# Three loads of second token weights are issued ahead of the last row loads, in the prologue of a Fourier filter with an MLP mixer

## The chip, the cores and the metric

The kernel runs on one core of one Trainium2 chip, as a single launch. The metric is the device time in microseconds (us), the median of several executions. A core has five engines, each with its own instruction queue that is worked off in order: PE (matmuls, with weight loads shown as PEld), DVE (elementwise), ACT (elementwise, and it issues DMAs), POOL (elementwise, and it issues DMAs) and SP (it only issues DMAs). They wait for one another through semaphores. DMAs run beside them on 16 DMA engines; an issued DMA "lands" when its semaphore is set.

## What is computed

Inputs are x of 8 x 3008 x 256 and the weights, all 64-bit floats; the result is 32-bit. Cut to what matters:

```
y = irfft(rfft(x, axis=1) * (filt_r + 1j * filt_i))      # per batch and channel, 3008 points
xt = y.transpose(0, 2, 1)
h  = relu(xt @ w_tok1) @ w_tok2                          # 3008 -> 256 -> 3008, along the tokens
u  = y + h.transpose(0, 2, 1)
out = u + relu(u @ w_ch1) @ w_ch2                        # 256 -> 1536 -> 256, along the channels
```

## The kernel before

**Stages.** The transform of 3008 points is done as matmuls: step A with 64 points (`a_unit`), step B with 47 points (`b_unit`, L529), the product with the filter, and back (`bi_unit`, L553), whose results are stored to the DRAM tensor `g_tmp` (L571, issued by ACT). `t4_load` (L608) loads them back as rows, six tiles per batch. The token mixer multiplies all six with `w1` (`token_sums`, L613, matmuls of L617), applies the relu (`token_relu`, L629) and multiplies with `w2` (`u_unit`, L642, matmuls of L647). The channel mixer (`mix`, L846) then runs for eight batches, with the filter of the next batches woven in. Batch 0 is filtered first, alone, in the prologue; the prologue ends where the mixer starts, about 153 us into a span of 2573.1 us.

**The weights.** They arrive as 64-bit floats and are turned into 32-bit ones on the chip, in 38 tiles: 0 to 11 hold `w_tok1`, 12 to 25 hold `w_tok2` (L329; tiles 18 and 25 have 188 columns, the others 471, and 128 partitions of 8 bytes a number), 26 to 37 hold the channel weights. Each tile passes four steps, in the order of the tiles: *begin* (the load into a staging buffer `st`, L337, issued by POOL), *copy* (ACT, L262), *middle* (DVE, L264 and L265), *end* (DVE, L268 and L270, after which the staging buffer is free; for tiles 12 to 17 PE then sums the two halves by L303 and L304 and ACT copies them out by L306, for later tiles DVE sums them by L292). `convert_middle` (L411) does one middle, and then issues the PE sums that are left; `convert_end` (L415) does one end, the copies that are due, and calls `fill(5)`: it begins tiles until there are five more begun than ended. While the list `pause` is not empty, `fill` begins none.

**The order around the change.** The order on each engine is that in which the program is written. The loop at L937 runs the filter of batch 0; each of its steps k does one middle or one end (L952 to L957) and some row loads, as their part of `g_tmp` becomes ready. From k = 27 on the loads are paused (L951); 18 tiles (0 to 17) are begun by then. The loop leaves with 16 tiles ended and 17 middles done. Then stand the last row loads (L967 and L968): the last 16 rows of each of the six tiles, 64 KB each, three on SP and three on POOL. They wait for the last store to `g_tmp`. Then the pause is lifted (L969), and the loop at L974 goes on with the tiles: i = 16 does middle 17, end 16, and begins tiles; i = 17 does middle 18, end 17, begins a tile, and then writes the PE sums that are left (`sum_up`) and `token_sums(0)`. So on DVE the first half of tile 18 (L264, L265) stands ahead of the second half of tile 17 (L268, L270), and on PE the sums of tile 17 (L304) stand ahead of `token_sums`. After the loop come `token_relu` and `u_unit` (L980 to L984).

**Buffers.** Tiles 18, 19 and 20 are staged in the buffers that tiles 12, 13 and 14 used, so their loads wait for L270 of those tiles. Tiles 21 to 25 follow in the buffers of 15 to 19.

Of the kernel before, what the change touches and what calls it, by code (L numbers as in the profile page):

```python
# [127 lines left out]
def kernel(  # L128
# [273 lines left out]
    def sum_up():  # L402
        while behind:
            behind.pop(0)()

    def convert():

        convert_middle()
        convert_end()

    def convert_middle():  # L411
        advance(middle)
        sum_up()

    def convert_end():  # L415
        ended[0] += 1
        advance(end)
        copies()
        fill(5)
# [3 lines left out]
    def copies():  # L423

        while copied[0] < len(tiles) and copied[0] <= ended[0] + (copied[0] < len(tiles) - len(LAST)):
            advance(copy)
            copied[0] += 1

    begun, pause = [0], []

    def fill(ahead):
        while not pause and begun[0] < len(tiles) and begun[0] < ended[0] + (4 if begun[0] >= len(tiles) - len(LAST) else ahead):
            start()

    def start():
        advance(begin)
        begun[0] += 1
# [26 lines left out]
    def rows_of(t_d, b):  # L464
        return t_d[b].rearrange("k (g a) d -> (k g) a d", a=A)
# [142 lines left out]
    def t4_load(b, c, lo=PARTS[0], hi=P, queue=nc.sync):  # L608
        if lo == 0:
            t4[b, c] = t4p.tile([P, TC4, D], FP32, tag="t4", name="t4")  # L610
        queue.dma_start(t4[b, c][lo:hi], rows_of(g_d, b)[lo:hi, ts(c, TC4), :])

    def token_sums(b):  # L613
        acc = bank(free_bank()).rearrange("p (t d) -> p t d", t=TC)
        for a in range(A):
            for t in range(TC):
                nc.tensor.matmul(acc[:, t, :], w1[:, a, ts(t, P)], t4[b, a // TC4][:, a % TC4, :],  # L617
                                 start=(a == 0 and t == 0), stop=(a == A - 1 and t == TC - 1))
        return acc

    def token_relu(b, acc):
        if b:
            h1 = w2[:, 0:1, 7 * 256:].rearrange("p o (s t) -> p o s t", t=P)[:, :, 0:7, :]
            for t, to in enumerate((slice(0, 5, 4), slice(1, 7, 5))):
                nc.scalar.activation(out=h1[:, 0, to, :], in_=acc[:, t].rearrange("p (e i) -> p e i", e=DH), func=AF.Relu)
            combine(h1)
            return h1[:, 0]
        h1 = h1p.tile([P, TC, D], FP32, tag="h1", name="h1")
        nc.scalar.activation(out=h1, in_=acc, func=AF.Relu)  # L629
        return h1  # L630
# [194 lines left out]
    def u_part(b, m, i):  # L825
        if i == 0:
            uts[b, m] = up.tile([P, DH, 512], FP32, tag="u", name="u")
        (u_quarter if b else u_unit)(b, m, h1s[b], uts[b, m], i)

    def v_steps(b, m):  # L830
        vts[b, m] = vp.tile([P, 4, 256], FP32, tag="v", name="v")
        t13, t2, t4_ = u_sums(uts[b, m], vts[b, m], width(m))

        def t24():
            t2()
            t4_()

        return [t13, t24]
# [91 lines left out]
    with tc.manual_schedule():  # L930
        nc.sync.dma_start(wa0, wa0_d)
        nc.vector.memset(turned[:, A:K2, :], 0.0)
        for t in filts:
            nc.vector.memset(t, 0.0)
        half = 0
        second = dft(GROUPS[1])
        for i, _ in enumerate(dft(GROUPS[0])):  # L937
            if i == 0:
                nc.scalar.dma_start(wai_t, wait_d)
            k = i - NXC - 2  # L940

            if i < NXC:
                if i in (1, 3, 5, 7, 9):
                    start()
                if i == NXC - 1:
                    copies()
                    for t, src in ((wa, wa_d), (wai, wai_d), (ident, ident_d)):
                        nc.scalar.dma_start(t, src)
            elif k >= 0:
                if k == K2 - 5:  # L950
                    pause.append(True)  # L951
                while half < 2 * IN_B * (k + 1) // K2:  # L952
                    if half % 2:
                        convert_end()
                    else:
                        convert_middle()
                    half += 1  # L957

                if 19 <= k < 25:
                    t4_load(0, k - 19, 0, PARTS[1])  # L960
                elif 26 <= k < 29:
                    for c in range(2):
                        t4_load(0, 2 * (k - 26) + c, PARTS[1], PARTS[2])
                elif k in (30, 31):
                    for c in range(3):
                        t4_load(0, 3 * (k - 30) + c, PARTS[2], PARTS[3])
        for c in range(A // TC4):  # L967
            t4_load(0, c, PARTS[3], P, (nc.sync, nc.gpsimd)[c % 2])  # L968
        pause.clear()  # L969
        both = wcp.tile([P, 2, JP, 7, P], FP32, tag="wc", name="wc")  # L970

        chan.extend((both[:, 0], both[:, 1]))
        next(second)
        for i in range(IN_B, A // 2 + TC * W2G):  # L974
            convert()
            if i == A // 2 + BY_PE - 1:
                sum_up()
                acc = token_sums(0)

        ahead[0](XF, nc.gpsimd)  # L980
        h1s[0] = token_relu(0, acc)
        for dh in range(DH):
            convert()
            u_part(0, 0, dh)  # L984
        for f in v_steps(0, 0):
            f()
        for _ in range(XB):
            next(second)
        group, todo, done = -1, iter(()), True

        def next_ready(b):
            return done or b != GROUPS[group][-1]

        left, places, at, spread = K2 + 3, 2 * 24, 0, True
        for b, i, place in mix(next_ready):
            if group + 1 < len(GROUPS) and b == GROUPS[group + 1][0]:
                if not done:
                    raise AssertionError("the filter's steps don't fit beside the mixer's")  # L1000
                group += 1
                done = group + 1 == len(GROUPS)
                todo = iter(()) if done else dft(GROUPS[group + 1]) if group else second
            due = place == 1
            if group == 0:
                due = spread
                if not spread and place:
                    at += 1
                    due = at * left // places > (at - 1) * left // places or at > places
            if due and not done:  # L1010
                spread = next(todo, "end")
                done = spread == "end"
# [30 lines left out]
```

## Time and profile before

| what | value |
|---|---|
| median of 9 runs | 2577.27 us (2572.84 to 2579.93) |
| profiled execution | 2575.04 us, of which its span is 2573.1 us |
| PE busy | 2490.7 us, 97% of the span |
| DVE busy | 1920.1 us, 75% |
| ACT, POOL busy | 680.0 us, 592.0 us |
| mean granted PE clock | 0.992 |
| DMA | 248.37 MB, 97 GB/s on average; 220 GB/s between 60 and 180 us |

The span is the time from the first to the last instruction. Three more views are used below. The chain of waits follows the work that ended last back, at each step to what released it; its lines are start, duration and what. The timeline lists each engine's instructions: start, duration, engine, line of the code, operation, output<-input and shape, and in brackets the idle time before it and who ended that. The table of windows gives, for each stretch of time, its length, the busy time (and count) of PE, PEld, DVE, ACT and POOL, then the granted PE clock, the mean busy share of the DMA engines, and GB/s.

### The profile page before, as it was taken

What the parts mean: (1) busy time and instruction counts of PE and PEld (TensorE: products, weight loads), DVE (VectorE), ACT (ScalarE), POOL (GpSimd) and SP (SyncE); (2) the same over time, 40 slices, a digit from 0 to 9 for tenths busy, and PEclk for the clock granted to TensorE, in tenths of its full rate; (3) what the DMA queues carried; (4) which work ended last, traced back from release to release, by engine and by line L of the source; (5) the groups of instructions that cost most, each with busy time, mean ns of one, the idle gap of its engine ahead of it and who ended that gap; (6) DMA issues with size and microseconds to landing.
All of it is one profiled execution on the core that took longest, in us unless ns stands there. A gap on an engine that the chain in (4) does not pass through costs nothing.

```text
span 2573.1 us, 32285 instructions
## 1 busy us (share of the span) xinstructions
PE 2490.7 (97%) x11204; PEld 2050.3 (80%) x11204; DVE 1920.1 (75%) x3594; ACT 680.0 (26%) x1342; POOL 592.0 (23%) x1073
## 2 busy tenths in 40 slices
PE   7889999999999999999999999999999999999997
PEld 3567666888888777898888777898888888898887
DVE  7687888567686998756776899856788587757776
ACT  5633222122221222222221222212222122212222
POOL 5573322212111121112121111211211121211222
PEclk8999999999999999999999999999999999999999
DMA  9873434333332333213332343213333222111100
GB/s 222 233 211 125 136 113 130 105 110 101 124 103 80 91 107 87 78 56 120 101 109 86 89 119 96 89 33 110 101 105 94 66 76 71 40 32 37 43 14 20
DMA packets 166432, 248.37 MB, mean 97 GB/s; under 512 B 35300, under 2 KB 112474, under 8 KB 166270
## 3 DMA queue, kind: packets, MB, share of 16 engines
q1 hardware_dynamic: 93006, 150.24, 19.6%
q0 software_dynamic: 33312, 48.47, 7.5%
q10 hardware_dynamic: 39952, 47.61, 5.8%
q8 instruction: 89, 1.46, 0.2%
q14 instruction: 73, 0.60, 0.1%
HBM read 168.96 MB, written 77.22 MB: 96 GB/s over the span
## 4 chain that ended last, share of the span: by engine, by line
PE 73%; DVE 17%; DMA 3%; ACT 3%; issue 2%; POOL 1%; ACTq 1%; DVEq 0%; SPq 0%; POOLq 0%
PE ps_po L774 25%; PE ps_pg L740 15%; PE ps_pg L756 10%; PE ps_b L617 4%; DVE t L718 4%; DVE hh L718 3%; PE ps_acc L661 2%; PE ps_b L661 2%; PE ps_acc L617 2%; DVE u L718 2%; DVE s L718 2%; PE ps_acc L639 2%; PE ps_b L639 2%; PE ps_b L560 1%; PE ps_b L535 1%
## 5 line engine op out<-in xcount | busy, mean ns | idle before, releaser
L819 POOL DMA_DIRECT2D out_dram<-r x757 | 411.9, 553 | 1756.2 <-ACT t L566 705.2
L718 DVE TENSOR_TENSOR hh<-ps_pg,s 128x512 f32<-128x512 f32 (+3 forms) x864 | 482.8, 586 | 343.8 <-ACT s L743 336.0
L761 ACT ACTIVATE hh<-hh 128x512 f32<-128x512 f32 (+1 forms) x576 | 347.8, 621 | 1198.1 <-DVE hh L718 1198.1
L774 PE MATMUL ps_po<-t,wc 128*128 128x256 f32 (+1 forms) x2304 | 535.9, 375 | 6.6 <-DVE t L718 5.7
L774 PEld LDWEIGHTS ps_po<-t,wc 128*128 128x128 f32 x2304 | 433.9, 190 | 132.1 <-issue 52.9
L740 PE MATMUL ps_pg<-v,wc 128*128 128x256 f32 (+1 forms) x1728 | 414.4, 376 | 2.5 <-DVE v L718 2.4
L774 PE MATMUL ps_po<-hh,wc 128*128 128x256 f32 (+1 forms) x1728 | 412.8, 375 | 0.2 <-ACT hh L761 0.2
L740 PEld LDWEIGHTS ps_pg<-v,wc 128*128 128x128 f32 x1728 | 328.2, 190 | 42.8 <-DVE v L718 5.1
L774 PEld LDWEIGHTS ps_po<-hh,wc 128*128 128x128 f32 x1728 | 328.4, 190 | 38.1 <-ACT hh L761 0.5
L756 PE MATMUL ps_pg<-u,wc 128*128 128x256 f32 (+1 forms) x1152 | 293.4, 377 | 8.6 <-DVE hh L718 8.3
L718 DVE TENSOR_TENSOR t<-t,hh 128x256 f32<-128x256 f32 (+1 forms) x576 | 246.3, 428 | 19.8
L756 PEld LDWEIGHTS ps_pg<-u,wc 128*128 128x128 f32 x1152 | 216.2, 190 | 44.7 <-DVE hh L718 19.5
L718 DVE TENSOR_TENSOR s<-ps_pg,hh 128x512 f32<-128x512 f32 (+1 forms) x288 | 196.1, 681 | 30.0
L718 DVE TENSOR_TENSOR t<-hh 128x512 f32<-128x512 f32 (+1 forms) x288 | 193.1, 670 | 0.6 <-ACT hh L761 0.6
L743 ACT COPY s<-ps_pg 128x256 f32<-128x256 f32 (+1 forms) x288 | 106.0, 368 | 315.4 <-PE ps_pg L740 309.3
L740 PE MATMUL ps_pg<-u,wc 128*128 128x256 f32 (+1 forms) x576 | 169.2, 375 | 2.7 <-DVE hh L718 2.7
L756 PE MATMUL ps_pg<-v,wc 128*128 128x256 f32 (+1 forms) x576 | 168.9, 375 | 0.0
L740 PEld LDWEIGHTS ps_pg<-u,wc 128*128 128x128 f32 x576 | 109.0, 190 | 28.1 <-issue 11.0
L756 PEld LDWEIGHTS ps_pg<-v,wc 128*128 128x128 f32 x576 | 108.7, 190 | 13.1
L718 DVE TENSOR_TENSOR u<-ps_acc,u 128x512 f32<-128x512 f32 (+3 forms) x105 | 61.1, 582 | 76.5 <-PE ps_acc L661 60.1
L617 PE MATMUL ps_b<-t,w 128*128 128x256 f32 x480 | 105.7, 382 | 1.1 <-ACT t L566 1.1
L718 DVE TENSOR_TENSOR u<-ps_b,u 128x256 f32<-128x256 f32 (+3 forms) x105 | 59.5, 566 | 61.0 <-PE ps_b L661 42.4
(132 smaller groups left out, 2526.4 us busy)
## 6 DMA issues: line engine op xcount, KB each, us to landing
w<-w_tmp SPq DMA_DIRECT2D x35, 896.0 KB
g_tmp<-t ACTq DMA_DIRECT2D x128, 192.0 KB
out_dram<-r POOLq DMA_DIRECT2D x698, 32.0 KB, 1.8
z_tmp<-t ACTq DMA_DIRECT2D x84, 256.0 KB
t<-z_tmp SPq DMA_DIRECT2D x112, 192.0 KB
t<-g_tmp SPq DMA_DIRECT2D x42, 512.0 KB
wb<-wbi_t SPq DMA_DIRECT2D x80, 224.0 KB
x<-in_x_dram SPq DMA_DIRECT2D x139, 128.0 KB
```

The source lines that it names most:

```text
L535: nc.tensor.matmul(ps, wbs[k // WC][0:P if first else KR, k % WC, 0:P], t2, start=True, stop=True)
L560: nc.tensor.matmul(ps[0:KR], wi, p, start=(i == 0), stop=(i == len(parts) - 1))
L617: nc.tensor.matmul(acc[:, t, :], w1[:, a, ts(t, P)], t4[b, a // TC4][:, a % TC4, :], start=(a == 0 and t == 0), stop=(a == A - 1 and t == ...
L639: nc.tensor.matmul(ps[:, ds(q * P, n)], t4[b, c][:, r, ts(dh, P)], wai[:, 0:n], start=(first and q == 0), stop=(not first and q == 3))
L661: nc.tensor.matmul(ps[:, ds(j * hw, hw)], h1[:, n, :], w2m[m % 2][:, at, 0:hw], start=(i < 2 and j == 0), stop=(j == len(todo) - 1))
L718: nc.vector.tensor_tensor(out=out, in0=in0, in1=in1, op=op)
L740: nc.tensor.matmul(ps[:, 0:hw], chan[0][:, jp, n, :], mov, start=True, stop=True)
L743: nc.scalar.copy(out=s[:, 0], in_=g[0][:, 0, 0:hw])
L756: nc.tensor.matmul(ps[:, 0:hw], chan[0][:, jp, n, :], mov, start=True, stop=True)
L761: nc.scalar.activation(out=hs, in_=hs, func=AF.Relu)
L774: nc.tensor.matmul(po[i][:, j, 0:hw], chan[1][:, jp, n, :], mov, start=(jp == 0 and first == 1), stop=(jp == JP - 1 and last == 1))
L819: q.dma_start(rows[g, e, :, ds(h * A + 4 * m, n)], blocks[ts(g, CW), h, e, 0:n])
```

## The change

`pause.clear()` moves ahead of the loop of the last row loads, and a call of `fill(5)` is put between the two. With 16 tiles ended, it begins tiles up to 21, so the loads of tiles 18, 19 and 20 (188 KB, 471 KB and 471 KB) stand on POOL ahead of its three row loads instead of behind them. Every later `fill` finds the same number of tiles begun as before or begins the fewer that are left: the loads of tile 21 and after stay behind the row loads, in the same order. No other engine's instructions change places, and none is added or removed.

```
--- before
+++ after
@@ -964,9 +964,11 @@
                 elif k in (30, 31):
                     for c in range(3):
                         t4_load(0, 3 * (k - 30) + c, PARTS[2], PARTS[3])
+        pause.clear()
+
+        fill(5)
         for c in range(A // TC4):
             t4_load(0, c, PARTS[3], P, (nc.sync, nc.gpsimd)[c % 2])
-        pause.clear()
         both = wcp.tile([P, 2, JP, 7, P], FP32, tag="wc", name="wc")
```

More of the change, by code (lines that the diff above doesn't have):

```diff
@@ L966 @@
                         t4_load(0, 3 * (k - 30) + c, PARTS[2], PARTS[3])
+        pause.clear()
+        fill(5)
         for c in range(A // TC4):
             t4_load(0, c, PARTS[3], P, (nc.sync, nc.gpsimd)[c % 2])
-        pause.clear()
         both = wcp.tile([P, 2, JP, 7, P], FP32, tag="wc", name="wc")
```

## The prediction

> **What bounds the kernel now.** I read first the shares of the chain that ended last, on the page. PE holds most of it, but DVE, DMA and ACT have their parts, so a stall can be removed only where the chain leaves PE.
>
> ```profile
> PE 73%; DVE 17%; DMA 3%; ACT 3%; issue 2%; POOL 1%; ACTq 1%; DVEq 0%; SPq 0%; POOLq 0%
> ```
>
> Then I read that chain in order of time around the moved loads (104 to 126 us).
>
> ```profile
> 110.41 2.12 DMA g_tmp<-t
> ...
> 114.31 0.48 POOL t L611
> ...
> 114.85 4.64 DMA st<-in_moe_w_tok_dram
> ...
> 119.56 0.38 ACT both L262
> ...
> 119.97 0.27 DVE both L264
> ...
> 120.96 0.66 DVE both L270
> ...
> 121.67 1.94 PE ps_po L304 x2
> 123.61 2.52 PE ps_b L617 x7
> ```
>
> The reader is to see a detour. The last store to g_tmp lands at 112.53, POOL issues its row loads, and only then asks for tile 18 (114.85). That load, not the rows, holds up everything: ACT copies tile 18, DVE does its middle, then the end of tile 17 that stands behind it, then PE sums tile 17 (L304), and only then can token_sums (L617) start. The timeline shows the idle time that this leaves, on DVE and on POOL, and when the three staging buffers had become free:
>
> ```profile
> 92.29 0.65 DVE L270 SCALAR_TENSOR_TENSOR both<-st,both 128x471 f32<-128x471 uint32 x1
> ...
> 99.65 0.65 DVE L270 SCALAR_TENSOR_TENSOR both<-st,both 128x471 f32<-128x471 uint32 x1
> ...
> 104.93 0.65 DVE L270 SCALAR_TENSOR_TENSOR both<-st,both 128x471 f32<-128x471 uint32 x1
> ...
> 112.10 0.65 DVE L270 SCALAR_TENSOR_TENSOR both<-st,both 128x471 f32<-128x471 uint32 x1
> 119.97 0.26 DVE L264 TENSOR_SCALAR both<-both 128x188 uint32<-128x188 uint32 x1 [7.22 <-ACT both L262]
> ```
>
> ```profile
> 113.12 1.67 POOL L611 DMA_DIRECT2D t<-g_tmp  x3 [12.71 <-DMA g_tmp<-t]
> 114.85 2.71 POOL L337 DMA_DIRECT2D st<-in_moe_w_tok_dram  x5
> ```
>
> The first three lines are the ends of tiles 12, 13 and 14: their buffers are free at 92.9, 100.3 and 105.6. POOL meanwhile sat 12.71 us in front of a row load. The fourth and fifth show DVE idle for 7.22 us, from the end of tile 16 to the middle of tile 18. The windows show the other costs:
>
> ```profile
> 100.00:105.00 5.00, 5.00 (x18) 3.34 (x17) 3.02 (x7) 4.14 (x9) 0.42 (x1) 0.84 0.90 244
> 105.00:110.00 5.00, 4.99 (x20) 3.21 (x19) 4.14 (x8) 4.53 (x9) 0.00 (x0) 1.00 0.49 119
> 110.00:115.00 5.00, 4.20 (x10) 1.45 (x9) 2.64 (x6) 1.38 (x3) 1.67 (x4) 1.00 0.38 97
> 115.00:120.00 5.00, 0.00 (x0) 0.00 (x0) 0.03 (x1) 0.44 (x2) 2.56 (x5) 0.87 1.04 213
> 120.00:125.00 5.00, 3.33 (x6) 2.17 (x7) 3.60 (x10) 2.79 (x5) 1.08 (x2) 0.50 1.04 386
> ```
>
> PE does nothing from 115 to 120 and then runs at a granted clock of 0.50, while the DMA engines, 0.38 to 0.49 busy from 105 to 115, are full (1.04) from 115 to 125. The work is there, in the wrong half of that stretch.
>
> **The change, part by part.** It adds no instruction. It moves three DMA issues on POOL (0.54 to 0.56 us each by the row of L337, together 1.6 us) ahead of three row loads; no other queue, SP's and ACT's included, changes its order.
>
> *When are the three loads issued now?* POOL's last filter load ends at 100.4. Tile 18 then waits for nothing (its buffer is free since 92.9) and goes out at about 101, tile 19 at about 101.5 (buffer free at 100.3), tile 20 at about 106 (105.6). Behind tile 20 stand only the row loads, which can't go before 112.56 anyway: the added wait on POOL costs nothing, with 6.5 us to spare. From issue to landing the loads of L337 took 3.3 to 8.1 us, 4.9 at the median. At the worst, tiles 18, 19 and 20 are there at 109, 109.6 and 114.1, and tile 18 is wanted at 112.75, tile 20 not before the copies of 18 and 19.
>
> *What goes.* DVE's idle 7.22 us ahead of the middle of tile 18. It starts at 112.75, when the end of tile 16 is done.
>
> *What is late next, on PE.* From L264 to L304 the chain takes 121.67 - 119.97 = 1.70 us, so DVE allows L304 at 114.45. PE is at L303 until 114.55 (it starts there at 113.69, and two matmuls of this shape hold the chain for 0.86 at full clock). L304 then takes 0.86 instead of 1.94, and token_sums can start at 115.4 instead of 123.61: 8.2 us earlier. It needs the last rows of its first tile, which SP asked for from 112.61 on. SP's landings aren't listed; POOL's row loads landed after 3.2 to 3.9 us. By those the rows are there at 115.8 to 116.5, so the start moves by 7.1 to 8.2. Its second tile comes by POOL, issued at 113.12 and landed by 117.0, and is wanted 16 matmuls (3.5 us) after the start: no wait. The 96 matmuls took 21.75 us with part of them at the clock of 0.50; at the later rate of 1.73 us for 8 such (L774) they take 20.76, 1.0 us less. What is left of PE's idle time is at most 2 us in two pieces, against the 7.02 that preceded the low clock, so I count on that 1.0 us. On PE the relu comes 8.1 to 9.2 us earlier.
>
> *What is late next, on DVE.* From 119.97 to 144.56 DVE worked nearly without a pause (4.76 to 4.83 us of each 5) on tiles 17 to 25, and u_unit needs the last of them. That stretch moves by 7.22 and becomes the later one: it ends at 137.3, against the relu at 136.8 to 137.9. The first L647, at 146.02 before, starts at 137.4 to 138.0: 8.0 to 8.6 us earlier. But the channel weights that follow on DVE, and POOL's sums behind them, move by 7.2 alone, so behind the start of the mixer I count 7.2 to 8.0 and take 7.5.
>
> *Is DVE fed?* Tile 21 is the first load behind the rows, issued at 114.85. DVE wants it copied when tile 20 is done, at 128.03 - 7.7 = 120.3 (7.22, and half a microsecond because ACT no longer waits for L304), so landed by 119.65. With the 4.64 us that tile 18 took in this very place it lands at 119.5, with the median 4.9 at 119.75, with the worst 8.1 at 122.95. That is 0 to 3.3 us of stall; I take nothing, since both near rows give 0 to 0.1, and keep 3.3 for the range.
>
> *What do the early loads take from others?* 1130 KB move into 101 to 112 us. There run the last filter loads (the one that the chain waits for lands at 104.91), the stores to g_tmp and the row loads of SP. The filter loads are on the same POOL queue and ahead of the tiles. A lower bound is nothing: from 105 to 115 more than half of the DMA time is unused. An upper bound is that all three tiles go first: 1130 KB at the 220 GB/s of 60 to 180 us are 5.3 us. The nearest row is the window of 105 to 110 (share 0.49), so I take nothing, and keep 5.3.
>
> A rule that speaks against this: the Trainium skill (DMA: Bandwidth & Descriptors, section "Queues, rings and completion order") says that each DMA engine takes turns between the queues it has work for, a packet at a time. By it a tile asked for early is not behind the stores but shares every turn with them. With its fit in "Anatomy of one DMA" (2.0 us plus the bytes at 436 GB/s) tile 20, issued at 106, would be through at about 109, an estimate, ahead of the last store at 110.41, and the sum would stay. The trace has no tile load beside a last store, so no row decides this; the measured 3.3 to 8.1 us say that the fit is too quick here.
>
> *Sum.* Of the profiled execution (2575.04 us, with 1.94 outside the span): 2575.04 - 7.5 = 2567.5. The median of the runs is 2.23 us above that execution, so for the median 2577.27 - 7.5 = **2569.8 us**. Behind 200 us PE is busy to 97% and every wait hangs on other work of the kernel, not on a date, so I see nothing to swallow a shift as a whole.
>
> **Rivals.**
> *The tiles delay the filter loads and stores that the rows wait for.* For it: the share of 0.90 in 100 to 105. Against it: 0.49 and 0.38 behind that. Price up to 5.3: a gain of 2.2, 2575.1 us.
> *DVE starves on tile 21.* For it: five loads are queued together behind the rows, and SP's x loads run in 115 to 120 too. Price up to 3.3: a gain of 4.2, 2573.1.
> *The gain is given back in the early mixer.* Between 150 and 330 us ACT waits for stores to z_tmp three times, 10.2 us together, and the chain has one store of 7.37 us at 165. If the earlier start runs into the same congestion at the same date, up to 7.37 is lost: 2577.1.
> *Slower.* The same mechanism, with the last store to g_tmp as its place: were the tiles to hold back that store and with it all row loads, the point from which it decides is a delay of 7.5 us, and for more than 0.2% of time (5.15 us; about what a measurement of this kernel can tell from no change) it must be 12.7. The three tiles would have to run at 90 GB/s, about the least that any of these windows shows (97), with nothing beside them. At 14 us: 2583.8.
> *It does nothing.* If the three loads found their buffers taken until 112. The ends of tiles 12 to 14 speak against it: 2577.3.
>
> **How the numbers follow.** Forecast 0.68 (a gain of 5.2 to 9.5: 2567.8 to 2572.1), filter loads delayed 0.08, starved 0.08, given back 0.07, nothing 0.02, slower 0.07. A third of "starved" still gains over 5.15, hence faster 0.71, same 0.22, slower 0.07. The range runs from 2566.0 (9.2 on every engine, and 2 for the scatter of medians) to 2576.5 (with most of the four small cases); outside it I leave 0.15 to 0.2.
>
> **What would show it.** In the profile after: the three L337 on POOL between 101 and 107 and its L611 still near 113; no idle line of 7 us on DVE ahead of the L264 with 188 columns; L617 starting at 115 to 117 and lasting 20.8; a clock of 1.00 in 115 to 125; the first L647 near 138. The prediction is wrong if the last L611 is issued later than 113.9 by several us, if L262 waits for st again at tile 21, or if L740, first at 153.15 before, comes 7.5 us earlier and the end doesn't.

## The result, and the profile after

The changed kernel takes 2569.43 us (median of 9 runs, 2566.9 to 2571.21), the kernel before, run beside it, 2577.64 us (29 runs): a ratio of 0.9968 [0.9959, 0.9976], 8.2 us faster. The forecast was 2569.8. Its profiled execution took 2570.3 us, of which its span is 2568.3.

The shares of the chain that ended last, on the page of the changed kernel: PE has 3 points less and DVE 2 more.

```profile
PE 70%; DVE 19%; DMA 3%; issue 3%; ACT 3%; POOL 1%; ACTq 0%; DVEq 0%; POOLq 0%; SPq 0%
```

The chain of waits of the changed kernel, in order of time, where the detour by tile 18 was:

```profile
115.70 3.36 DMA g_tmp<-t
...
120.86 0.46 POOL t L611
...
121.39 5.72 DMA st<-in_moe_w_tok_dram
...
127.85 0.42 DVE both L264
...
138.27 4.70 DMA st<-in_moe_w_ch_dram
...
152.49 0.87 POOL wc L360
```

It looks the same at first: store, row loads, a tile, DVE. But the tile of 121.39 is now tile 21, not 18, and the path goes on over DVE and POOL to the channel weights, for which PE waits just behind its first L740 (153.40 below); `token_sums` is no longer on it. The timeline of the changed kernel shows what each engine did (DVE, then POOL, then PE):

```profile
113.24 0.68 DVE L543 TENSOR_TENSOR p<-ps_pg,filt 128x512 f32<-128x512 f32 x1
...
117.97 0.26 DVE L264 TENSOR_SCALAR both<-both 128x188 uint32<-128x188 uint32 x1
...
127.85 0.41 DVE L264 TENSOR_SCALAR both<-both 128x471 uint32<-128x471 uint32 x1 [2.18 <-ACT both L262]
```

```profile
105.66 1.12 POOL L337 DMA_DIRECT2D st<-in_moe_w_tok_dram  x2
111.12 0.54 POOL L337 DMA_DIRECT2D st<-in_moe_w_tok_dram  x1 [4.34 <-DVE both L270]
119.64 1.69 POOL L611 DMA_DIRECT2D t<-g_tmp  x3 [7.98 <-DMA g_tmp<-t]
```

```profile
121.75 20.96 PE L617 MATMUL ps_b<-t,w 128*128 128x256 f32 x96 [1.02 <-issue]
143.60 1.99 PE L647 MATMUL ps_acc<-w,h 128*128 128x512 f32 x4 [0.90 <-ACT h L629]
...
150.74 0.59 PE L740 MATMUL ps_pg<-u,wc 128*128 128x256 f32 x2
153.40 1.56 PE L740 MATMUL ps_pg<-v,wc 128*128 128x256 f32 x6 [2.07 <-POOL wc L360]
```

The line with 188 columns, tile 18's middle, has no bracket: DVE no longer waits 7.22 us for it. Instead it waits 0.90 at tile 19 (not among these lines) and 2.18 at tile 21. POOL asks for tiles 18 and 19 at 105.66, for 20 at 111.12, and still stands idle for 7.98 before the rows. The windows of the changed kernel (columns as before: length, PE, PEld, DVE, ACT, POOL, clock, DMA share, GB/s) follow. Its prologue came 5.2 us later in this profile, as is explained next, so each window is read against the one that begins 5 us earlier in the kernel before. The DMA engines are 1.00, 0.72 and 0.58 busy where they were 0.90, 0.49 and 0.38, and in 120 to 125 PE works for 3.98 us at a clock of 1.00, where it did nothing in 115 to 120:

```profile
105.00:110.00 5.00, 5.00 (x16) 3.16 (x16) 2.88 (x7) 4.02 (x8) 1.78 (x4) 0.77 1.00 299
110.00:115.00 5.00, 4.81 (x20) 3.04 (x19) 3.86 (x8) 4.11 (x9) 0.54 (x1) 1.00 0.72 205
115.00:120.00 5.00, 4.55 (x12) 1.91 (x11) 4.39 (x10) 2.77 (x6) 0.36 (x1) 1.00 0.58 124
120.00:125.00 5.00, 3.98 (x17) 2.92 (x16) 4.28 (x11) 1.90 (x4) 3.36 (x7) 1.00 0.98 180
```

**How to compare the two traces.** Put side by side, the dates mislead: the first L740 moved only from 153.15 to 150.74, 2.4 us, while the runs gained 8.2. Three more profiles of the kernel before explain it. This is the timeline of one of them (DVE): the last product with the filter (L543), at 108.06 in the first profile of the same kernel, came 5.3 us later, and the wait for tile 18 is there all the same.

```profile
113.39 0.68 DVE L543 TENSOR_TENSOR p<-ps_pg,filt 128x512 f32<-128x512 f32 x1
...
125.41 0.26 DVE L264 TENSOR_SCALAR both<-both 128x188 uint32<-128x188 uint32 x1 [7.35 <-ACT both L262]
```

In 14 profiles this L543 begins between 108.06 and 115.40, whatever the kernel. The scatter arises earlier: the last filter load goes out 7.4 to 8.4 us before it in each of the 13 whose chain shows that load, and on POOL it stands ahead of every moved load. So I count all dates from this L543 (F). Behind the first L740 the kernels can't be told apart: from there to the end of the span it is 2417.8 to 2420.0 us in the four profiles of before, 2417.6 to 2419.0 in the three of after. The table gives the start of L617, of L647 and of L740 behind F, and the larger times lost on DVE ahead of the middles of second token weights (tile 19 in the kernel before: at most 0.27).

| kernel | ratio [interval] | DVE idle before L264 (tile) | L617 | L647 | L740 |
|---|---|---|---|---|---|
| before (4 profiles) | 1 | 7.2 to 7.4 (18), 1.0 to 1.2 (20) | 15.3 to 15.5 | 37.7 to 39.0 | 44.8 to 46.1 |
| after | 0.9968 [0.9959, 0.9976] | 0.90 (19), 2.18 (21) | 8.51 | 30.36 | 37.50 |
| after, again | 0.9963 [0.9951, 0.9975] | 0.91 (19), 0.83 (21) | 7.32 | 28.99 | 36.12 |
| after, third time | 0.9973 [0.9964, 0.9983] | 0.90 (19), 1.10 (21) | 7.72 | 29.37 | 36.49 |
| one tile early | 0.9991 [0.9982, 1.0] | 6.88 (19) | 7.32 | 33.93 | 42.44 |
| two tiles early | 0.9988 [0.9979, 0.9997] | 0.91 (19), 3.49 (20) | 7.32 | 31.76 | 40.56 |
| two, again | 0.9976 [0.9966, 0.9986] | 0.92 (19), 3.52 (20) | 7.37 | 31.66 | 38.80 |
| four tiles early | 0.9979 [0.997, 0.9988] | 0.92 (19), none behind | 9.05 | 30.70 | 37.82 |
| before, order swapped | 0.9995 [0.9986, 1.0004] | 6.43 (18), 1.19 (19) | 7.20 | 34.77 | 44.34 |
| after, order swapped | 0.9969 [0.9958, 0.9981] | 0.3 (19), 0.2 (20), 1.04 (21) | 7.31 | 28.95 | 36.08 |
| before, all rows on SP | 0.9982 [0.9973, 0.9991] | 1.71 (18), 0.2, 0.2 | 10.50 | 32.15 | 39.27 |

On the mean of its three profiles the changed kernel starts the mixer 36.70 us behind F, the kernel before (four) 45.45: 8.75 us earlier, for 8.2, 9.2 and 6.7 us of time in three comparisons.

### The profile page after: what moved, and what is told of

It reads as the page before. It is cut to its first block, busy times and chain, and to the rows that moved or that the text cites. A ratio compares the mean times of both kernels' runs of the same rounds, so it can differ in the third digit from the quotient of the medians.

```text
span 2568.3 us, 32282 instructions
## 1 busy us (share of the span) xinstructions
PE 2486.4 (97%) x11204; PEld 2047.5 (80%) x11204; DVE 1919.0 (75%) x3594; ACT 679.6 (26%) x1342; POOL 592.4 (23%) x1073
## 4 chain that ended last, share of the span: by engine, by line
PE 70%; DVE 19%; DMA 3%; issue 3%; ACT 3%; POOL 1%; ACTq 0%; DVEq 0%; POOLq 0%; SPq 0%
PE ps_po L774 24%; PE ps_pg L740 14%; PE ps_pg L756 10%; DVE t L718 4%; DVE hh L718 4%; PE ps_b L617 3%; PE ps_acc L661 2%; PE ps_b L661 2%; PE ps_acc L617 2%; DVE u L718 2%; DVE s L718 2%; PE ps_acc L639 2%; PE ps_b L639 2%; PE ps_acc L469 1%; PE ps_b L535 1%
## 5 line engine op out<-in xcount | busy, mean ns | idle before, releaser
L740 PE MATMUL ps_pg<-v,wc 128*128 128x256 f32 (+1 forms) x1728 | 413.1, 375 | 4.5 <-DVE v L718 2.4
L740 PEld LDWEIGHTS ps_pg<-v,wc 128*128 128x128 f32 x1728 | 327.4, 190 | 44.4 <-DVE v L718 5.1
L740 PE MATMUL ps_pg<-u,wc 128*128 128x256 f32 (+1 forms) x576 | 169.1, 375 | 3.7 <-DVE hh L718 3.7
L740 PEld LDWEIGHTS ps_pg<-u,wc 128*128 128x128 f32 x576 | 109.0, 190 | 28.7 <-issue 10.8
L617 PE MATMUL ps_b<-t,w 128*128 128x256 f32 x480 | 104.7, 380 | 2.1 <-ACT t L566 1.1
```

Of the source, the lines that this page charges most:

```text
L740: nc.tensor.matmul(ps[:, 0:hw], chan[0][:, jp, n, :], mov, start=True, stop=True)
```

## The experiments

My theory (A in the texts on record): the time follows the start of the mixer, which is set by the end of DVE's conversions together with `token_sums` and the relu on PE, so that what counts is that DVE is fed without a gap. The rivals: that the start of `token_sums` alone is what counts; that the difference is the scatter of the prologue; that the early tiles are paid for by the stores and rows beside which they run.

**The changed kernel again.** No edit.

> The changed kernel once more, for a second profile. In the first profile of it the last row loads went out at 119.6 us, 6.5 us later than before, though nothing ahead of the moved loads had changed. Theory C (chance): the filter loads of the prologue scatter from one execution to the next, and here POOL's first L611 comes anywhere between 112 and 120 us. Rival D (the early tile loads slow the last filter loads and stores): it comes at 118 to 121 again, and the last store to g_tmp takes over 3 us. The time is 2569.4 within 2 us in both.

Measured: 2567.46 against 2576.7, 0.9963 [0.9951, 0.9975]. POOL's first L611 comes at 115.89, as theory C allows and rival D doesn't. Its timeline (PE) has `token_sums` without a wait, and the whole gain:

```profile
117.79 20.88 PE L617 MATMUL ps_b<-t,w 128*128 128x256 f32 x96
139.46 1.99 PE L647 MATMUL ps_acc<-w,h 128*128 128x512 f32 x4 [0.79 <-ACT h L629]
```

**Only tile 18 early.** In the changed kernel:

```
-        fill(5)
+        fill(3)
```

> Only tile 18 (188 KB) goes ahead of the rows; tiles 19 and 20 stay behind them. The detour to token_sums is gone as in the changed kernel, but DVE runs dry on tile 19, whose load is asked for after the rows and lands about 5 us later. Theory A (the end of DVE's conversions decides): gain of 2 to 4 us, 2573.5 to 2575.5. Rival B (the start of token_sums decides): gain of 7 to 8, 2569.5 to 2570.5. In both, token_sums starts 2 to 3 us after POOL's last L611.

Measured: 2574.21, 0.9991 [0.9982, 1.0]. `token_sums` starts 7.32 behind F, as early as in the changed kernel, and yet only 2.5 us are gained: the gap has gone one tile on, to tile 19. Its timeline, DVE and then PE:

```profile
124.40 0.41 DVE L264 TENSOR_SCALAR both<-both 128x471 uint32<-128x471 uint32 x1 [6.88 <-ACT both L262]
```

```profile
145.07 3.37 PE L647 MATMUL ps_acc<-w,h 128*128 128x512 f32 x4 [5.72 <-ACT h L629]
```

PE is done with `token_sums` and then idle for 5.72 us, until the relu ends; in the kernel before and the changed one L647 follows L617 within 0.7 to 0.9 us, relu included. The relu itself takes 0.58 us, but it runs late: on ACT it stands behind the copies of the tiles, and the last of these waits for DVE's sums. The timeline of ACT:

```profile
143.87 0.66 ACT L262 ACTIVATE both<-st 128x512 f32<-128x512 f32 x1 [1.82 <-DVE w L292]
144.44 0.58 ACT L629 ACTIVATE h<-ps_b 128x512 f32<-128x512 f32 x1
```

So DVE's pace holds L647 here, by way of ACT's queue. In the four profiles of the kernel before it is the other way round: there the relu waits 1.7 to 3.0 us for `token_sums`, so PE was the later path and DVE close behind.

**The order swapped in the kernel before.** At L974, so that the end of tile 17 doesn't stand behind the middle of tile 18; no load is moved:

```
-            convert()
+            if i == A // 2 + BY_PE - 1:
+                convert_end()
+                convert_middle()
+            else:
+                convert()
```

> The kernel before with its loads in the old places, but with the end of tile 17 written ahead of the middle of tile 18, so that token_sums waits no longer for the load of tile 18, while the conversions of tiles 18 to 25 come as late as before. Theory A (the end of DVE's conversions decides): gain of 1 to 2.5 us, 2575 to 2576.5, with L617 starting 7 to 8 us earlier against POOL's L611 and the first L647 waiting for DVE's L292. Rival B (the start of token_sums decides): gain of 7 to 8 us, about 2570.

Measured: 2576.31, 0.9995 [0.9986, 1.0004]. This removes the detour itself, and next to nothing comes of it: 0.4 us, and the interval includes no change. Its timeline, PE and then DVE:

```profile
117.77 20.88 PE L617 MATMUL ps_b<-t,w 128*128 128x256 f32 x96
145.34 3.78 PE L647 MATMUL ps_acc<-w,h 128*128 128x512 f32 x4 [6.68 <-ACT h L629]
```

```profile
122.68 0.26 DVE L264 TENSOR_SCALAR both<-both 128x188 uint32<-128x188 uint32 x1 [6.43 <-ACT both L262]
```

L617 comes 8.3 us earlier behind F and the mixer 1.1: an earlier start of `token_sums` alone brings little, as long as DVE stands still for 6.43 us. PE's wait has moved behind L617, for the relu again stands behind ACT's copies. L647 still comes 3.6 us earlier than in the kernel before, but 2.4 of these are lost up to the first L740: the granted clock is 0.50 in 145 to 150 us, and the four L647 take 3.78 us instead of 1.98.

**Rows on SP alone, in the kernel before.** At L968:

```
-            t4_load(0, c, PARTS[3], P, (nc.sync, nc.gpsimd)[c % 2])
+            t4_load(0, c, PARTS[3], P)
```

> The kernel before with all six last row loads on SP, so that POOL has none and its tile loads wait for nothing but their buffers; the pause is lifted where it was. If the cause is that the tile loads stand in POOL's queue behind a load that waits for the last store, this gains as much as the change: 7 to 8 us, about 2570, and 1 to 2 us more if tile 21, which then also comes early, was short in the changed kernel (ACT waited 5.0 us for it there): 2568. Rival D (bytes beside the last stores and rows cost): less than the change gains, 2571 to 2574, since four to five tiles are then in flight beside them.

Measured: 2572.47, 0.9982 [0.9973, 0.9991]. With no row load to wait for, POOL begins tiles as their buffers come free, and half of the gain is there: 4.2 us of time, with the mixer 39.27 behind F, 6.2 earlier. The time lies in rival D's range. The rest is lost on the rows. Its timeline, ACT's last store and SP's last loads:

```profile
116.44 0.31 ACTq L571 DMA_DIRECT2D g_tmp<-t  x1
```

```profile
120.10 2.77 SPq L611 DMA_DIRECT2D t<-g_tmp  x6
```

The first of the six rows goes out 3.66 us after the store's issue (2.20 in the kernel before), and issuing six on one queue takes 2.77 us instead of 1.23 for three; `token_sums` starts at 10.50 behind F. How much each of the two costs was not separated.

**Two tiles early**, `fill(4)` in place of `fill(5)`; and once more, as the first comparison showed a smaller gain than its trace:

> Tiles 18 and 19 go ahead of the rows, tile 20 behind them. Theory A (the end of DVE's conversions decides): each tile more ahead of the rows moves the place where DVE runs dry one tile (about 3 us of DVE's work) back, so the idle time of 6.9 us that one tile left shrinks to about 4, and the gain is 4.5 to 6 us: 2571 to 2572.5. Rival B' (two tiles already bring the whole gain, because only the detour to tile 17 and one tile of stock matter): 8 us, 2568.5. The last store to g_tmp: between 2.1 us (no or one early tile) and 3.4 (three).

> Two tiles ahead of the rows, once more, beside the changed kernel. In the first profile of it the stretch from DVE's last product with the filter (L543) to the mixer (L740) was 40.6 us, 5 less than in the kernel before (45.1 and 46.1), but the median had gained only 2.6. Theory C (the date of L543 scatters by chance, 114.2 in that profile): the stretch is 40.6 within 1 us again, and the time comes nearer to a gain of 5: 2571 to 2573. Rival D' (an early load always costs some us ahead of L543): the gain stays at 2.6 within 1, and L543 comes at 113 or later again.

Measured: 2574.33, 0.9988 [0.9979, 0.9997], and 2571.82, 0.9976 [0.9966, 0.9986]. DVE's gap is now at tile 20 and is 3.5 us long in both. The gains are 2.6 us, less than theory A's 4.5 to 6, and 5.5 us; the mixer starts 4.9 and 6.7 earlier.

**Four tiles early**, `fill(6)`:

> Tile 21 too goes ahead of the rows. DVE no longer starves there (it stood 2.2 us in one profile of the changed kernel), but 471 KB more run beside the last store and the row loads, and token_sums can't start earlier. Theory A with the relu as the next bound (in the second profile of the changed kernel the first L647 waited for the relu alone): the same time as the changed kernel within 1.5 us, 2567 to 2570. Rival D (bytes beside the last store cost): the store takes 4 us or more, token_sums starts later, and 1 to 3 us of the gain go: 2569.5 to 2572.

Measured: 2571.54, 0.9979 [0.997, 0.9988]. DVE has no gap behind tile 19, but nothing more is gained: the time lies in rival D's range, not in theory A's. The relu waits 2.46 us for `token_sums` again, which starts at 9.05. Its timeline, ACT's last store, then POOL:

```profile
114.88 0.31 ACTq L571 DMA_DIRECT2D g_tmp<-t  x1
```

```profile
114.66 0.54 POOL L337 DMA_DIRECT2D st<-in_moe_w_tok_dram  x1 [4.75 <-ACT both L262]
119.59 1.68 POOL L611 DMA_DIRECT2D t<-g_tmp  x3 [4.40 <-DMA g_tmp<-t]
```

The fourth tile goes out beside the last store, and POOL gets its first row load off 4.71 us after the store's issue. That interval is 2.70 to 2.71 with no or one early tile, 2.70 and 2.94 with two, 2.94 to 3.94 with three. So early tiles do slow the store. The Trainium skill's rule that the engines take turns between queues (DMA: Bandwidth & Descriptors, "Queues, rings and completion order") fits this; no run shows the turns themselves. By the mixer's start four tiles lose 1.1 us to the mean of three, and 0.3 to the latest of its profiles; the intervals of the times overlap.

**The changed kernel with the order swapped too**, same edit as above:

> The changed kernel with the end of tile 17 ahead of the middle of tile 18 as well. DVE's work up to tile 17 ends about 0.6 us earlier; the landing of the rows, not PE's sums, then sets the start of token_sums. Theory A: no change against the changed kernel, 2568.5 within 1.5 us. If the PE sums of tile 17 still held token_sums up, 0.5 to 1 us less.

Measured: 2569.55, 0.9969 [0.9958, 0.9981], L740 36.08 behind F: no more than the change alone.

**Repeats.** The kernel before three times, one execution each, and the changed kernel a third time, no edit:

> The kernel before once more, for a second profile of it. Theory C (the prologue's filter loads scatter by chance): DVE's last product with the filter (L543), at 108.1 us in the first profile, falls anywhere between 107 and 114, as it did in the others (110.6 without any moved load, 110.5 to 113.3 with). From it, token_sums starts 15 us later and the mixer (L740) 45 us later, within 1.5 us, in both profiles. Rival D (only moved loads delay it): 108 again within 1 us.

> The kernel before, a third profile: L543 to L740 45 to 46.5 us, L617 15 to 16 us behind L543. Under C its L543 comes later than 111 in at least one of this and the next profile; under D' it is at 108 to 111 in both, as in the first two.

> The kernel before, a fourth profile: the same as for the third.

> The changed kernel a third time, beside the run with two tiles. L543 to L740 takes 36 to 38 us, the time is 2567.5 to 2569.5. Under C its L543 lies anywhere between 108 and 116, under D' at 113 or later.

Measured: 2575.55, 2579.05 and 2577.25 us, with DVE idle for 7.40, 7.35 and 7.42 us ahead of tile 18; and 2570.59, 0.9973 [0.9964, 0.9983]. F comes at 113.39 without any moved load and at 109.72 with two, so a late F is not the mark of moved loads. The scatter explains the dates, not the gain: the two kernels stay apart when counted from F. One doubt is left. The five profiles without early tiles have F at 110.5 on the mean, the nine with them at 112.5, and in eight of the ten comparisons the time gained is 0.5 to 2.3 us less than the mixer's advance behind F. In all nine the last filter load goes out ahead of the first early tile's load, so I take this for scatter, but it is not shown.

## Why the prediction was right

- *The idle time ahead of tile 18 goes.* Shown: 7.2 to 7.4 us in four profiles of before, none in three of after.
- *The added wait on POOL costs nothing.* Shown: POOL still idled 7.7 to 8.0 us ahead of its rows in three profiles, against the 6.5 predicted to spare.
- *`token_sums` starts 7.1 to 8.2 earlier and takes 20.76 us.* Behind F it went from a mean of 15.46 to 8.51, 7.32 and 7.72: 7.0 to 8.1 earlier. It took 20.88 to 20.96 us in all three, and 21.5 to 22.8 in the four before.
- *First L647 8.0 to 8.6 earlier.* Means behind F: 38.3 and 29.6, a little more than predicted. The prediction tied it to DVE by the last tile that `u_unit` needs. But in the changed kernel it starts at 143.60, ahead of DVE's last sums for tile 25 (143.93); what ties it to DVE is the relu's place behind ACT's copies, as the run with one tile shows.
- *The mixer 7.2 to 8.0 earlier, taken as 7.5.* This term was too small by 1.2 us: 8.75 was measured. It is the path over PE, and it adds up: on the means `token_sums` starts 7.61 earlier and takes 1.25 less, the pause up to L647 grows by 0.10, and from L647 to the first L740 it is 7.12 to 7.14 in all seven profiles. The prediction let the weights converted on DVE hold the mixer to 7.2. They came only 6.3 earlier (middle of tile 25, 31.9 behind F on the mean before, 25.6 after): the gaps of 7.3 at tile 18, 1.1 at tile 20 and 0.2 at tile 19 went, and gaps of 0.9 at tile 19 and 0.8 to 2.2 at tile 21 came. "Nearly without a pause" overlooked the second and third of these, though its own window of 120 to 125 shows DVE busy for 3.60 of 5 us. But the weights held only a part of the mixer: behind its first two L740 PE waits 2.0 to 2.4 us for L360, so that the next six come 6.6 earlier, and the group after these is 8.7 earlier again.
- *DVE is fed at tile 21, taken as 0, bound 3.3.* It was not quite: 2.18, 0.83 and 1.10 us. The trace shows why in the run with 2.18: the load was issued at 121.39, behind rows that the store had delayed, and took 5.72 us, not 4.64.
- *The early loads take nothing, bound 5.3.* True for the filter: the last filter load took 4.9 to 5.6 us in before and 5.3 to 5.6 in after, and F follows it in the same 7.7 to 8.4 us. Not for the last store: POOL's rows follow it 0.2 to 1.2 us later, and L617 came up to 1.2 later than the earliest. The nearest row that I chose, the window with a share of 0.49, showed room for the tiles, and the matching window with them is not full (0.72); the store became slower all the same.
- *The fit of the Trainium skill* (DMA: Bandwidth & Descriptors, "Anatomy of one DMA", 2.0 us plus the bytes at 436 GB/s) gives 3.1 us for 471 KB, an estimate. In 100 to 126 us of the changed kernel the tiles took 5.7 at the median and 10.2 at the most: too quick by far when several are queued.
- *Given back in the early mixer.* False: from the first L740 to the end it is 2417.3 to 2420.0 us in all 14 profiles. The wait of 2.07 us for channel weights (L360) just behind the first L740 is not visible in the sum.
- *The signs given for "wrong".* Two of the three came, and the forecast held. The last L611 was issued later than 113.9 by several us (the three go out from 119.64 on): this sign was badly made, a date from the start of the span, where it should be counted from F. And ACT's L262 waited for `st` again at tile 21, for 5.02 us in the first profile, of which DVE lost 2.18.

That the forecast of 2569.8 lies 0.4 us from the 2569.43 measured is partly luck. The three comparisons gave 8.2, 9.2 and 6.7 us, 8.0 on the mean; the term's error of 1.2 us is smaller than their spread, and part of it does not appear in the time.

The gain is thus shown to need both paths, and the moved loads serve both. With `token_sums` as early as 7.2 to 7.4 us behind F, the mixer starts at 44.3 with no tile early (the swapped order), at 42.4 with one, at 40.6 and 38.8 with two and at 36.1 with three, while DVE's gap goes from tile 18 to 19 to 20 to 21 and shrinks; with four it is away. The low clock's part of the 8.75 is some 2.1 us by these lengths: the 1.25 by which `token_sums` takes less, and 0.9 ahead of it, where the two L304 take 1.06 us instead of 1.94. Besides the doubt about F, one thing stays open: whether not pausing the loads at all (L951) would do the same. By the program's text it would let POOL begin these tiles ahead of its rows too, but it wasn't tried.

## What to carry to other kernels

A queue that issues in order should get what has its buffer free before what must still wait for a store; count how many loads the consumer needs until the next can arrive, for each one short left a gap one tile sooner here (6.9 us with one tile early, 3.5 at two, 0.8 to 2.2 at three), and one too many ran beside the store that is waited for. Where two chains meet (here PE's sums and DVE's conversions), an earlier start of one brings little while the other has the gap; and a short instruction, here the relu, can be late only because of what stands ahead of it in its queue. Compare single profiles from the last event ahead of the change, not from the start.

## What was not expected of the hardware

The same kernel's prologue scatters by 5.3 us (F at 108.06 to 113.39 in the four profiles of before), while from the first L740 to the end the same four profiles agree within 2.2 us. And the low clock outlasts the idle time by an amount that differs: the same 96 matmuls took 21.5 to 22.8 us in these four. The windows of the one with 22.8 (the second of the four) show it: PE is busy throughout the second, and still gets 0.59.

```profile
120.00:125.00 5.00, 1.52 (x2) 0.84 (x3) 2.97 (x8) 1.87 (x3) 0.54 (x1) 0.50 1.01 350
125.00:130.00 5.00, 5.00 (x15) 3.89 (x14) 3.69 (x9) 1.91 (x3) 1.02 (x2) 0.59 0.75 289
```

The two profiles with two tiles early differ in their clock too. PE is idle for 3.56 us ahead of L647 in the one and for 3.33 in the other; then the four L647 take 2.84 and 2.00 us, and the window of 145 to 150 us has a clock of 0.69 in the one, that of 140 to 145 us a clock of 1.00 in the other.
